# Attention, routing and mixing in one kernel: fewer idle products in the attention, the values' router products a turn later, their weights loaded in the setup, and the counts' product two steps later

## The chip, the cores and the metric

The kernel runs on one core of a Trainium2 chip. The engines have short names in all that follows: PE is TensorE (matmuls; PEld its weight loads), DVE is VectorE, ACT is ScalarE, POOL is GpSimd, SP is SyncE, which here only issues DMAs. The metric is the device time of one execution in microseconds, lower is better; the median of several runs counts.

## The reference

Three layers follow each other: an attention with a local window, a few global keys and a bias by distance; a layer of experts in which each token takes one of eight, chosen by a router, or keeps that of the token before it; and a mixer (a Fourier transform over sequence and channels, a normalization, two matmuls). Cut to what matters here:

```python
# q, k, v: (2, 8, 768, 64) f32; n_global = 8, n_local = 96
scores = (q @ k.T) / 8 + bias                 # bias = -slope[head] * distance
a = softmax(where(is_global | is_local, scores, -1e9))
x = (a @ v), heads joined to rows of 512      # (2, 768, 512)

logits = x @ w_gate                           # (2, 768, 8)
local_gate = sigmoid(x @ w_local)
for s in range(768):                          # in each sequence
    e = argmax(logits[s]) if s == 0 or local_gate[s] < 0.5 else previous e
    out[s] = softmax(logits[s])[e] * (relu(x[s] @ w1[e]) @ w2[e])

u = out + real(fft2(out));  result = u + relu(norm(u) @ w_ch1) @ w_ch2
```

## The kernel before, in words

The program issues everything by hand in a fixed order. `setup` loads the constants, `fast_attention` does the attention and, in between its work, the routing; the experts and the mixer follow. Only the attention is touched.

The sequence is cut into six tiles of 128 queries, numbered i. A unit is four heads of one sequence for one tile: 24 units, and the main loop over n starts one unit in each turn. A turn is a software pipeline over four units:

- scores of unit n (PE, L152, tile `sp`), their smallest value with the bias added (DVE, L161), the exponentials (ACT, L169);
- some idle products (PE, L50, `keep_busy`), multiplications of zeros that nobody reads, as many as the list `BUSY` says;
- transposes of unit n-1 (PE, L178, tile `tp`) in two halves, each copied out of PSUM by ACT (L184, tile `p`);
- values of unit n-2 (PE, L192, tile `op`), that is the attention's output before it is divided by the row sums;
- the division for unit n-3 (DVE, L204 to L209, `norm`).

Tile 0 sees only itself, so its scores are 128 wide and it has half the transposes and values; all later units take two tiles of keys. The buffers of `tp` are two, and idle products take one of them in turn. `op` is one.

The router's product x @ w_gate is not made from x. `prep_v` multiplies the transposed values with the router's weights (PE, L100, tiles `vt` and `wg`, into the small PSUM tile `sm`), and ACT copies the result (L103) beside the values in `vs`, so that the values product L192 gives the router's logits in ten more columns. It does so once for each tile of keys and in two halves, one for each sequence. So L192 for a tile waits for its L103.

The bias is a table that ACT writes (L229) from distances that DVE makes: eight rows 128 wide for tile 0 (`near`), eight rows 256 wide for all others (`far`).

Work beside the pipeline runs as generators: `bg.step()` stands four times in each turn and lets each live generator run on to its next `yield`. The routing of a tile (`Route.run`) is one of them: the logits, their largest, the scan over tokens that resolves "keeps the expert before" (L519), the scan that counts the tokens of each expert (L529, tile `cu`), and on PE the product of the counts (L534, `other`), from which DVE takes each token's rank (L541), PE the place (L546, L547), and POOL and SP write the rows and the list. For tile 3 the list is also read back, and a first group of tokens gathered, for an early start of the first expert (L828 and following).

A last generator halves expert weights for fast products (ACT L994, DVE L996) in some turns from 12 on.

Of the kernel before, what the change touches and what calls it, by code (L numbers as in the profile page):

```python
# [11 lines left out]
F32 = mybir.dt.float32  # L12
# [11 lines left out]
P = 128  # L24
# [3 lines left out]
NT = S // P  # L28
# [6 lines left out]
LIST = B * S  # L35
NL = E + 2
LAST = E - 1
BUSY = [6, 6, 4, 2, 2, 2, 2, 2, 2, 2] + [0] * 6
VC = D + NL + 1
BUBBLE = 0  # L40
GATE = -1.5 * 2.0 ** -23
# [4 lines left out]
def keep_busy(nc, st, ps, n):  # L46

    x = st.busy
    for _ in range(n):
        nc.tensor.matmul(ps, x[:, :1].to_broadcast([P, P]), x.unsqueeze(1).to_broadcast([P, 8, D]), start=True, stop=True)  # L50
# [10 lines left out]
def fast_attention(tc, st, io, route):  # L61
    nc = tc.nc
# [3 lines left out]
    with ExitStack() as ctx:  # L66
# [5 lines left out]
        ps_t = pool("ps_t", 2, space=PSUM)  # L72
# [15 lines left out]
        def load_v(i):  # L88
            nc.sync.dma_start(vs[:, i % KS], io["v"][i])

        def load_vt(i):
            vts[i] = raw.tile([P, HP, P], F32, name="vt", bufs=2)
            nc.sync.dma_start(vts[i], io["vT"][i])

        def prep_v(i):
            vt = vts.pop(i)
            for g in range(2):
                ps = route.sm[:, 80 + 80 * (i % 2):][:, :8 * NL]
                for k in range(4):
                    T.matmul(ps[:, k * 2 * NL:(k + 1) * 2 * NL], vt[:, 4 * g + k], route.wg[:, k, :2 * NL], start=True, stop=True)  # L100
                yield
                yield
                A.copy(vs[:, i % KS, 8 * g:8 * g + 8, D:VC - 1], ps.rearrange("p (h e) -> p h e", h=8))  # L103
                yield
            if i == 0:
                yield
                yield
                nc.sync.dma_start(gv, vs[:GMAX, 0])
# [167 lines left out]
        for n in range(N + 3):  # L276
            if ok(n):
                i, b, g = units[n]
                first = (b, g) == (0, 0)
                if (b, g) == (0, 1) and 0 < i < NT - 1:  # L280
                    load_vt(i + 1)
                if (b, g) == (1, 0) and 0 < i < NT - 1:
                    load_v(i + 1)
                if n == 1:
                    bg.add(prep_v(0))
                if i + 1 < NT and (b, g) == (1, 1):
                    bg.add(prep_v(i + 1))
                if first and i > 0:
                    load_kq(nc, st, io, i + 3)
                if (b, g) == (1, 0) and i >= 2:  # L290

                    st.ring.load(i - 2)
            if n == 1:
                bg.add(far())
            k = 4 * (n - N)
            if ok(n - 2):
                out(n - 2, 1)
            if ok(n - 3):
                norm(n - 3)
            if ok(n):  # L300
                scores(n)
                rowmin(n)
                if units[n][2]:
                    patch_k(*units[n][:2])
            step(k)
            if n < 2 * len(BUSY):
                keep_busy(nc, st, ps_t.tile([P, 2, 2, P], F32, name="tp").rearrange("p a b n -> p (a b n)"), BUSY[n // 2])
            if ok(n - 1):
                transp(n - 1, 0)
            if ok(n):  # L310
                expo(n)
            if ok(n - 1):
                out(n - 1, 0)
            step(k + 1)
            if ok(n - 1):
                transp(n - 1, 1)
            step(k + 2)
            if ok(n - 2):
                values(n - 2)
            step(k + 3)  # L320
            if ok(n - 3) and units[n - 3][2]:
                patch_v(*units[n - 3][:2])
            if n == 2:
                G.tensor_copy(gk, st.kq[0][:, 0, :, :GMAX])
            if ok(n - 3):
                live.pop(n - 3)
# [110 lines left out]
class Route:  # L437
# [3 lines left out]
    def pools(self, ctx, turn=True):  # L441
        tc = self.tc
        self.sb = ctx.enter_context(tc.tile_pool(name="rt", bufs=2))
        ps = ctx.enter_context(tc.tile_pool(name="ps_r", bufs=1, space=PSUM))
        one = ctx.enter_context(tc.tile_pool(name="rt_one", bufs=1))
        self.none = one.tile([P, (E * LIST + P) * 2 // P], I32, name="none")
        self.wg = one.tile([P, 4, 3 * NL], F32, name="wg")
        self.identb = one.tile([P, P], BF16, name="identb")
        tc.nc.scalar.dma_start(self.wg, self.io["wg"])

        self.tp = ps.tile([P, 4, P], F32, name="xtp") if turn else None
        self.sm = ps.tile([P, 512], F32, name="sm")
        return ctx.enter_context(tc.tile_pool(name="rtx", bufs=6))

    def run(self, i, xs, parts=None):
        nc, st, sb = self.tc.nc, self.st, self.sb
        V, A, G, T = nc.vector, nc.scalar, nc.gpsimd, nc.tensor
        tp, sm = self.tp, self.sm
# [71 lines left out]
                             op0=ALU.mult, op1=ALU.add)  # L530
        st.pe, st.pc = ex, cu
        yield

        T.matmul(other, from1, cu[:, P - 1:], start=i == 0, stop=True)  # L534
        if i == NT - 3:
# [218 lines left out]
def setup(tc, ctx, io):  # L754
    nc = tc.nc
    st = State()
    c = ctx.enter_context(tc.tile_pool(name="const", bufs=1))
    w = ctx.enter_context(tc.tile_pool(name="stage", bufs=1))
    st.raws = w.tile([P, PIECES, PW], F32, name="raws")
    st.raw = [st.raws[:, n] for n in range(PIECES)]  # L760

    st.kq = [t.rearrange("p (k h s) -> p k h s", k=2, h=B * H // 2) for t in st.raw]
    nn = c.tile([P, 4], I32, name="nn")
    nc.sync.dma_start(nn, io["nn"].to_broadcast([P, 4]))
    cs = c.tile([P, sum(CONSTS.values())], F32, name="consts")
    nc.scalar.dma_start(st.raw[3][:, 1024:1024 + 3 * P], io["masks"][:, :3 * P])
    nc.scalar.dma_start(cs, io["consts"])
    warm = c.tile([1, 1], F32, name="warm")
    nc.vector.memset(warm, 0.0)
    nc.scalar.activation(warm, warm, AF.Exp)  # L770
    o = 0
    for n, k in CONSTS.items():
        setattr(st, n, cs[:, o:o + k])
        o += k
    st.nf = c.tile([P, 4], F32, name="nf")
    V = nc.vector
    words = nn.rearrange("p (a b) -> p a b", b=2)
    lo, hi = st.nf[:, 0:2], st.nf[:, 2:4]
    V.tensor_copy(lo, words[:, :, 0])
    V.tensor_copy(hi, words[:, :, 1])  # L780
    V.scalar_tensor_tensor(hi, lo, 0.0, hi, op0=ALU.is_lt, op1=ALU.add)
    V.scalar_tensor_tensor(lo, hi, 2.0 ** 32, lo, op0=ALU.mult, op1=ALU.add)
    V.tensor_scalar(st.nf[:, 2:4], lo, -1.0, None, op0=ALU.mult)

    st.fast = c.tile([1, 1], I32, name="fast")
    f = c.tile([1, 2], F32, name="fastf")
    V.tensor_scalar(f[:, 0:1], st.nf[:1, 0:1], float(GMAX), None, op0=ALU.is_le)
    V.tensor_scalar(f[:, 1:2], st.nf[:1, 1:2], float(LMAX), None, op0=ALU.is_le)
    V.tensor_tensor(f[:, 0:1], f[:, 0:1], f[:, 1:2], op=ALU.mult)
    V.scalar_tensor_tensor(st.fast, st.nf[:1, 1:2], 1.0, f[:, 0:1], op0=ALU.is_ge, op1=ALU.mult)  # L790
    m = st.misc
    st.first, st.eid = m[:, 0:1], m[:16, 1:2]
    sb = c.tile([16, 4], F16, name="selbase")
    st.sb, st.sel, st.base = sb, sb[:, 0:2], sb[:, 2:4]
    st.busy = c.tile([P, D], BF16, name="busy")
    nc.gpsimd.memset(st.busy, 0.0)
    st.nch = c.tile([1, E + 2], I32, name="nch")
    st.ent0 = c.tile([P, 2], I32, name="ent0")
    st.p0 = c.tile([P, 1], F32, name="p0")
    st.ones16 = m[:16, 6:7].to_broadcast([16, P])  # L800
    st.dest = c.tile([P, B * NT, 2], I32, name="dest")
    dr = ctx.enter_context(tc.tile_pool(name="dram", bufs=1, space=DRAM))
    st.xs = dr.tile([B * S, ROW], F32, name="xs")
    st.wm = dr.tile([FT // 2, P, PW], F32, name="wmf")
    st.gv = dr.tile([GMAX, B * H, VC], F32, name="gv")
    st.list = dr.tile([E * LIST + P, 2], I32, name="list")
    st.x2 = io["x2"] if "x2" in io else dr.tile([B * S, DM], F32, name="x2")
    st.ring = Ring(tc, st, io)
    st.ring.add(w, 2)
    st.wide = w.tile([P, 3, 2, PW], F32R, name="wide")  # L810
    st.ring.slots += [[st.wide[:, k, n] for n in range(2)] for k in range(3)]

    hi, lo = st.ring.slots[4]
    v = lambda t, o, k: t[:, o:o + k * P].rearrange("p (k s) -> p k s", k=k)
    st.xe = [v(t, 0, 4) for t in (hi, lo)]
    st.he = [v(t, 4 * P, 8) for t in (hi, lo)]
    st.hs = st.raw[3][:, :1024]
    st.ye = st.raw[3][:, 1024:1024 + DM]
    return st
# [991 lines left out]
```

## Time and profile before

| | us |
|---|---|
| median of three runs | 693.82 |
| the three runs | 688.61, 693.82, 697.11 |
| the profiled execution, its own time | 695.23 |
| its span, first to last instruction | 693.5 |

The profile is that of the one execution of 695.23 us. Its times are counted from the span's start. In the attention, turn 0 begins at 6.05 and the last scores (turn 23) at 126.36; the values of turn 23's unit end at 138.2, and the experts begin at about 164. A row of the timeline gives start, length, engine, line, operation, the tiles written and read, how many instructions are merged in the row, and in brackets how long the engine stood idle before it and what released it. A matmul of full f32 stands twice in the trace for each one in the program.

### The profile page before, as it was taken

What the parts mean: (1) busy time and instruction counts of PE and PEld (TensorE: products, weight loads), DVE (VectorE), ACT (ScalarE), POOL (GpSimd) and SP (SyncE); (2) the same over time, 40 slices, a digit from 0 to 9 for tenths busy, and PEclk for the clock granted to TensorE, in tenths of its full rate; (3) what the DMA queues carried; (4) which work ended last, traced back from release to release, by engine and by line L of the source; (5) the groups of instructions that cost most, each with busy time, mean ns of one, the idle gap of its engine ahead of it and who ended that gap; (6) DMA issues with size and microseconds to landing.
All of it is one profiled execution on the core that took longest, in us unless ns stands there. A gap on an engine that the chain in (4) does not pass through costs nothing.

```text
span 693.5 us, 9885 instructions
## 1 busy us (share of the span) xinstructions
PE 657.4 (95%) x3646; PEld 538.4 (78%) x3647; DVE 392.5 (57%) x931; ACT 272.0 (39%) x478; POOL 67.8 (10%) x82
## 2 busy tenths in 40 slices
PE   7999999887989999999998899999999999999997
PEld 3778787755878899888786588777878888888885
DVE  3366766651967787877146987788742131254112
ACT  3464655611655565655243343443111131132110
POOL 0001110213034123322010000000000000000000
PEclk8799999978999999999999889999999999999999
DMA  7536545145779978995244033344110010100001
GB/s 274 219 132 131 133 116 165 50 95 187 267 264 372 318 246 277 358 342 199 89 161 176 0 122 122 121 164 160 42 61 0 1 61 0 61 0 1 0 1 61
DMA packets 26095, 96.20 MB, mean 139 GB/s; under 512 B 7764, under 2 KB 8916, under 8 KB 18096
## 3 DMA queue, kind: packets, MB, share of 16 engines
q1 hardware_dynamic: 20288, 81.19, 35.2%
q0 software_dynamic: 4736, 10.56, 4.2%
q10 hardware_dynamic: 1008, 3.65, 1.4%
q8 instruction: 34, 0.56, 0.3%
q14 instruction: 29, 0.24, 0.1%
HBM read 84.75 MB, written 14.88 MB: 144 GB/s over the span
## 4 chain that ended last, share of the span: by engine, by line
PE 40%; DVE 9%; ACT 2%; issue 1%; DVEq 0%; ACTq 0%
PE h L1621 16%; PE acc L1636 5%; PE acc L1637 5%; PE acc L1635 5%; DVE dec L1020 1%; DVE dec L1022 1%; PE y L1127 1%; PE more L1177 1%; PE acc L1442 1%; PE h L1177 1%; PE more L1127 1%; PE acc L1456 1%; PE f L1587 1%; DVE dec L1018 1%; DVE dec L1016 1%
## 5 line engine op out<-in xcount | busy, mean ns | idle before, releaser
L1626 DVE SCALAR_TENSOR_TENSOR hl<-h,hh 128x512 fp32r<-128x512 f32 x48 | 33.1, 689 | 120.4 <-ACT hh L1625 120.4
L1625 ACT ACTIVATE hh<-h 128x512 fp32r<-128x512 f32 x48 | 28.7, 597 | 156.7 <-PE h L1621 151.8
L996 DVE TENSOR_TENSOR wide<-raws,wide 128x1024 fp32r<-128x1024 f32 (+2 forms) x46 | 50.4, 1110 | 23.4 <-ACT wide L994 23.4
L169 ACT ACTIVATE t<-t,nm 128x256 f32<-128x256 f32 (+1 forms) x96 | 39.2, 479 | 43.5 <-DVE nm L161 41.6
L994 ACT CAST wide<-raws 128x1024 fp32r<-128x1024 f32 (+2 forms) x46 | 43.1, 960 | 4.4 <-PE acc L1637 3.5
L192 PE MATMUL op<-vs,p 128*128 128x75 f32 x352 | 43.9, 278 | 1.0 <-DVE xrow L209 1.0
L192 PEld LDWEIGHTS op<-vs,p 128*128 128x128 f32 x352 | 42.4, 196 | 1.2 <-issue 1.1
L161 DVE CUSTOM_DVE_ANT_0 t<-sp,bias 128x256 f32<-128x256 f32 (+1 forms) x96 | 32.9, 398 | 18.3 <-PE sp L152 15.9
L1621 PE MATMUL h<-un0h,wide 128*128 128x512 f32 (+1 forms) x136 | 42.8, 380 | 0.4 <-ACT un0h L1397 0.4
L1636 PE MATMUL acc<-wide,hh 128*128 128x512 f32 x96 | 38.1, 397 | 0.0
L1635 PE MATMUL acc<-wide,hh 128*128 128x512 f32 x96 | 37.8, 394 | 0.0
L1637 PE MATMUL acc<-wide,hl 128*128 128x512 f32 x96 | 37.7, 393 | 0.0
L1147 PE MATMUL h<-xh,wide 128*128 128x256 f32 x192 | 28.0, 281 | 2.6 <-DVE hl L1151 2.4
L1621 PEld LDWEIGHTS h<-un0h,wide 128*128 128x128 f32 x136 | 25.0, 188 | 5.8 <-ACT un0h L1397 0.6
L1007 ACT ACTIVATE dec<-raws 128x1024 f32<-128x1024 f32 x18 | 20.5, 1139 | 20.4 <-DMA wmf<-dec 6.2
L184 ACT COPY p<-tp 128x512 f32<-128x512 f32 (+1 forms) x48 | 25.1, 538 | 7.0 <-PE tp L178 6.8
L1057 POOL DMA_INDIRECT xg<-xs,ent x23 | 26.3, 1145 | 14.2 <-issue 5.5
L1147 PEld LDWEIGHTS h<-xh,wide 128*128 128x128 f32 x192 | 24.9, 188 | 3.6 <-DVE hl L1151 2.8
L178 PE MATMUL tp<-consts,t 128*128 128x128 f32 x176 | 26.8, 288 | 0.0
L178 PEld LDWEIGHTS tp<-consts,t 128*128 128x128 f32 x176 | 21.1, 147 | 6.4 <-issue 1.6
L1621 PE MATMUL h<-un0l,wide 128*128 128x512 f32 (+1 forms) x68 | 25.9, 380 | 0.0
L1150 ACT ACTIVATE hh<-h 128x512 fp32r<-128x512 f32 x28 | 16.6, 597 | 23.2 <-PE h L1147 20.4
(440 smaller groups left out, 1626.8 us busy)
## 6 DMA issues: line engine op xcount, KB each, us to landing
raws<-we SPq DMA_DIRECT2D x30, 1024.0 KB
raws<-wm SPq DMA_DIRECT2D x17, 1024.0 KB
raws<-wmf SPq DMA_DIRECT2D x7, 1024.0 KB
wmf<-dec POOLq DMA_DIRECT2D x8, 512.0 KB, 8.4
vs<-v SPq DMA_DIRECT2D x6, 600.0 KB
xs<-xrow SPq DMA_DIRECT2D x12, 260.0 KB
vt<-vT SPq DMA_DIRECT2D x6, 512.0 KB
raws<-kq SPq DMA_DIRECT2D x3, 1024.0 KB
```

The lines of the kernel that those rows point to most:

```text
L161: V.tensor_tensor_reduce(out=u.t[:, x, :u.W], in0=u.sp[:, j, k, :u.W], in1=bias[:, 4 * u.g + x, u.b0:u.b0 + u.W], scale=-0.125, scalar=3.0 ...
L169: A.activation(u.t[:, x, :u.W], u.t[:, x, :u.W], AF.Exp, bias=u.nm[:, x:x + 1], scale=-1.0)
L178: T.transpose(u.tp[k][:, j, c], u.t[:, 2 * k + j, c * P:(c + 1) * P], st.ident)
L192: T.matmul(u.op[:, x], u.p[:, x, c], vs[:, ti % KS, u.h + x], start=c == 0, stop=c == len(tiles) - 1)
L994: (first or nc.scalar.copy)(hi[:, cs], raw[:, cs])
L996: (eng() if callable(eng) else eng or nc.vector).tensor_tensor(lo[:, cs], raw[:, cs], hi[:, cs].bitcast(F32), op=ALU.subtract)
L1147: T.matmul(ps[:, u], w[:, f], x[:, k], start=n == 0, stop=n == 11)
L1621: nc.tensor.matmul(ps[:, c], a[:, k], x[:, k, c], start=n == 0, stop=n == 11)
L1626: nc.vector.scalar_tensor_tensor(hl, ps, 0.0, hh.bitcast(F32), op0=ALU.max, op1=ALU.subtract)
L1635: T.matmul(acc[c], hh[:, cs], h2, start=first, stop=False)
L1636: T.matmul(acc[c], hh[:, cs], l2, start=False, stop=False)
L1637: T.matmul(acc[c], hl[:, cs], h2, start=False, stop=last)
```

## The change

Four edits go together.

- `BUSY` had one entry for two turns: six idle products in each of turns 0 to 3, four in turns 4 and 5, two in turns 6 to 19. Now it has one for each turn: four, four, two and two in turns 0 to 3, and none behind. That is 60 before and 12 now.
- `prep_v(0)`, the router products for tile 0's values, is started in turn 2 instead of turn 1.
- The router's weights are loaded in the setup by ACT's queue, into a free part of a staging tile and ahead of the constants, and POOL copies them to `wg` once the branch to the fast attention is taken. Before, ACT's queue loaded `wg` behind that branch.
- The routing of tiles 0 to 4 yields twice more between the scan of the counts and the product of the counts. A yield is one of the four background steps of a turn.

```diff
-BUSY = [6, 6, 4, 2, 2, 2, 2, 2, 2, 2] + [0] * 6
+BUSY = [4, 4, 2, 2]
...
-                if n == 1:
+                if n == 2:
                     bg.add(prep_v(0))
...
-            if n < 2 * len(BUSY):
-                keep_busy(nc, st, ps_t.tile([P, 2, 2, P], F32, name="tp").rearrange("p a b n -> p (a b n)"), BUSY[n // 2])
+            if n < len(BUSY):
+                keep_busy(nc, st, ps_t.tile([P, 2, 2, P], F32, name="tp").rearrange("p a b n -> p (a b n)"), BUSY[n])
...
-        tc.nc.scalar.dma_start(self.wg, self.io["wg"])
+        tc.nc.gpsimd.tensor_copy(self.wg, self.st.wg)
...
         st.pe, st.pc = ex, cu
         yield
+        if i < NT - 1:
+
+            yield
+            yield
 
         T.matmul(other, from1, cu[:, P - 1:], start=i == 0, stop=True)
...
     nc.scalar.dma_start(st.raw[3][:, 1024:1024 + 3 * P], io["masks"][:, :3 * P])
+
+    st.wg = st.raw[3][:, 1024 + 3 * P:][:, :12 * NL].rearrange("p (k n) -> p k n", k=4)
+    nc.scalar.dma_start(st.wg, io["wg"])
     nc.scalar.dma_start(cs, io["consts"])
```

On PE, before, from turn 1's scores to turn 2's first idle product (tp are the transposes, sm the router products; of the idle products, six in each turn, the first stands here):

```order
L152 MATMUL sp<-raws 128x128 x4
L100 MATMUL sm<-wg,vt 128x20 x4
L50 LDWEIGHTS busy
L50 MATMUL tp<-busy 128x512
...
L178 MATMUL tp<-consts,t 128x128 x4
L100 MATMUL sm<-wg,vt 128x20 x4
L152 MATMUL sp<-raws 128x128 x4
```

The same place now, from turn 1's scores to turn 3's:

```order
L152 MATMUL sp<-raws 128x128 x4
L50 LDWEIGHTS busy
L50 MATMUL tp<-busy 128x512
...
L178 MATMUL tp<-consts,t 128x128 x4
L152 MATMUL sp<-raws 128x128 x4
L100 MATMUL sm<-wg,vt 128x20 x4
...
L178 MATMUL tp<-consts,t 128x128 x4
L192 MATMUL op<-vs,p 128x75 x4
L100 MATMUL sm<-wg,vt 128x20 x4
L152 MATMUL sp<-raws 128x128 x4
```

The first router products moved from behind turn 1's scores to behind turn 2's, with turn 0's transposes now ahead of them, and their second half from before the first values to behind them.

On ACT, before, behind turn 0's exponentials up to the second half of the router's copies (bias<-vs are table rows, t<-t,nm exponentials, p<-tp copies of transposes, vs<-sm the router's copies):

```order
L229 ACTIVATE bias<-vs 128x128 x3
L169 ACTIVATE t<-t,nm 128x128 x4
L184 COPY p<-tp 128x2x128
L229 ACTIVATE bias<-vs 128x256
L103 COPY vs<-sm 128x8x10
L229 ACTIVATE bias<-vs 128x256 x2
L184 COPY p<-tp 128x2x128
L229 ACTIVATE bias<-vs 128x256
L169 ACTIVATE t<-t,nm 128x128 x4
L184 COPY p<-tp 128x2x128
L103 COPY vs<-sm 128x8x10
```

Now, from the same place up to the first of these copies:

```order
L229 ACTIVATE bias<-vs 128x128 x3
L169 ACTIVATE t<-t,nm 128x128 x4
L184 COPY p<-tp 128x2x128
L229 ACTIVATE bias<-vs 128x256 x3
L184 COPY p<-tp 128x2x128
L229 ACTIVATE bias<-vs 128x256
L169 ACTIVATE t<-t,nm 128x128 x4
L184 COPY p<-tp 128x2x128
L229 ACTIVATE bias<-vs 128x256 x2
L103 COPY vs<-sm 128x8x10
```

The router's first copy moved from ahead of turn 2's exponentials to behind them, with all but two of the eight wide table rows ahead of it.

On PE in turn 12, the counts' product (L534 before) for tile 1, in one piece of the difference:

```order
 L152 MATMUL sp<-raws 128x256 x4
-L50 LDWEIGHTS busy
-L50 MATMUL tp<-busy 128x512
-L50 LDWEIGHTS busy
-L50 MATMUL tp<-busy 128x512
 L178 MATMUL tp<-consts,t 128x128 x4
 L528 MATMUL sm<-cu,consts 16x1
 L178 MATMUL tp<-consts,t 128x128 x4
-L534 MATMUL sm<-cu,consts 16x1
 L192 MATMUL op<-vs,p 128x75 x8
 L152 MATMUL sp<-raws 128x256 x4
```

It left its place between transposes and values; in the new program it is line L538 and stands behind the scores of turn 13, ahead of that turn's transposes. The two products of the places (L546 and L547, now L550 and L551) went from between turn 13's transposes to behind its values.

## Rows read from the trace of the kernel before

**Rows 1.** The page's 40 equal slices of the span: the granted clock, tenths.

```profile
PEclk8799999978999999999999889999999999999999
```

**Rows 2.** Timeline of PE, turn 10 and the start of turn 11.

```profile
58.13 1.13 PE L152 MATMUL sp<-raws 64*128 64x256 f32 x8
59.19 0.60 PE L50 MATMUL tp<-busy 128*128 128x512 bf16 x2
59.63 1.04 PE L178 MATMUL tp<-consts,t 128*128 128x128 f32 x8
...
62.34 1.13 PE L152 MATMUL sp<-raws 64*128 64x256 f32 x8
```

**Rows 3.** Timeline of PE, the scores of turns 22 and 23.

```profile
122.53 1.14 PE L152 MATMUL sp<-kq 64*128 64x256 f32 x8
...
126.36 1.14 PE L152 MATMUL sp<-kq 64*128 64x256 f32 x8
```

**Rows 4.** Windows of turns 21 and 22: busy by engine (count), clock, DMA, GB/s.

```profile
116.94:122.53 5.59, 5.59 (x36) 4.34 (x35) 3.48 (x17) 2.99 (x7) 1.19 (x2) 0.70 0.79 259
122.53:126.36 3.83, 3.83 (x34) 3.38 (x33) 3.76 (x20) 2.86 (x8) 1.02 (x1) 1.00 0.01 1
```

**Rows 5.** Timeline of PE, the product of the counts in tiles 0 to 4.

```profile
51.56 0.20 PE L534 MATMUL sm<-cu,consts 16*16 16x1 f32 x2 [1.45 <-ACT vs L103]
...
72.51 0.20 PE L534 MATMUL sm<-cu,consts 16*16 16x1 f32 x2 [1.18 <-ACT vs L103]
...
93.50 0.20 PE L534 MATMUL sm<-cu,consts 16*16 16x1 f32 x2 [1.18 <-ACT vs L103]
...
114.65 0.20 PE L534 MATMUL sm<-cu,consts 16*16 16x1 f32 x2 [1.57 <-ACT vs L103]
...
132.74 0.20 PE L534 MATMUL sm<-cu,consts 16*16 16x1 f32 x2 [0.80 <-DVE cu L529]
```

**Rows 6.** Timeline of ACT at the second of these.

```profile
72.24 0.22 ACT L103 COPY vs<-sm 128x80 f32<-128x80 f32 x1
```

**Rows 7.** Timeline of all engines at the start.

```profile
5.87 0.34 ACTq L449 DMA_DIRECT2D wg<-wg  x1
...
8.04 0.23 POOL L324 COPY gk<-raws 128x64 f32<-128x64 f32 x1 [7.12 <-DMA raws<-kq]
...
10.33 1.26 ACT L169 ACTIVATE t<-t,nm 128x128 f32<-128x128 f32 x4
...
11.11 1.86 PE L100 MATMUL sm<-wg,vt 128*128 128x20 f32 x8 [2.30 <-DMA vt<-vT]
...
16.00 0.37 ACT L184 COPY p<-tp 128x256 f32<-128x256 f32 x1 [4.41 <-PE tp L178]
16.27 0.42 ACT L229 ACTIVATE bias<-vs 128x256 f32<-128x256 f32 x1
16.58 0.22 ACT L103 COPY vs<-sm 128x80 f32<-128x80 f32 x1
...
16.86 1.90 PE L100 MATMUL sm<-wg,vt 128*128 128x20 f32 x8 [0.47 <-ACT vs L103]
...
18.68 1.23 PE L152 MATMUL sp<-raws 64*128 64x128 f32 x8
...
22.38 1.06 PE L178 MATMUL tp<-consts,t 128*128 128x128 f32 x4
...
23.23 1.73 PE L192 MATMUL op<-vs,p 128*128 128x75 f32 x8
```

**Rows 8.** Windows of half a microsecond where the granted clock fell and rose, columns as above.

```profile
11.00:11.50 0.50, 0.39 (x2) 0.42 (x3) 0.45 (x2) 0.50 (x3) 0.00 (x0) 0.58 0.94 395
...
24.50:25.00 0.50, 0.50 (x5) 0.42 (x4) 0.00 (x0) 0.50 (x2) 0.00 (x0) 0.76 0.10 19
```

**Rows 9.** Timeline of PE, scores of turn 4, and of turn 21 at the low clock.

```profile
30.04 1.13 PE L152 MATMUL sp<-raws 64*128 64x256 f32 x8
...
116.94 2.08 PE L152 MATMUL sp<-kq 64*128 64x256 f32 x8
```

## The prediction, made before the changed kernel ran

> **What bounds the kernel now.** I read the page's slices first, then TensorE's (PE's) timeline through the attention turn by turn, then the windows of the same turns, then the waits, and last the start with all engines. A turn is one pass of the loop over n; the attention's turns 0 to 23 each start four heads. The slices show a clock that is near full except at the very start, around the fifth part of the span and at a few later places [rows 1]. Within the attention PE has hardly a gap: a plain turn is scores, two idle products, transposes, values, and the next scores follow at once, 4.21 us in all, of which the two idle products take 59.19 to 59.63, 0.44 us or 0.22 each [rows 2]. Turns from 20 on have no idle products already, and turn 22, the same work without them, takes 3.83 us [rows 3]; its window shows the clock at 1.00 (the 2.4 GHz level) and VectorE (DVE) busy 3.76 us of the 3.83 [rows 4]. So an idle product here is on the path, and what comes next behind PE is close.
>
> The second thing on PE's path is five waits, one per tile of queries, each before the product of the counts at L534: 1.45, 1.18, 1.18, 1.57 and 0.80 us [rows 5]. The row that ends the second is ScalarE's (ACT's) copy L103, which stands in its queue behind the four exponentials and a copy out of PSUM and ends at 72.46, just before 72.51 [rows 6]; the last is ended by the scan itself. After the fourth wait the granted clock of turn 21 is 0.70 and the turn takes 5.59 us [rows 4].
>
> The third is the start. PE stands still for 2.30 us before the first router product at 11.11 [rows 7], since the transposed values must land first; the granted clock drops there to the 1.2 GHz level and comes back at 24.7 [rows 8]. First values only at 23.23 [rows 7], and turn 4 begins at 30.04 [rows 9].
>
> **Idle products from turn 4 on.** Turns 4 and 5 lose four each, turns 6 to 19 two each: 36 x 0.22 = 7.9 us [rows 2]. The check is turn 22 against turn 10: 4.21 - 3.83 = 0.38 for two [rows 2, 3]. Nothing on PE hides them.
>
> **The counts' wait.** Two more background steps put the product behind the next turn's scores, some 2 us later on PE, and the longest wait was 1.57. What is queued behind it on PE (values, the next scores) no longer waits; what waits for it is the rank on DVE, the positions, the writes of rows and list, and these have turns to spare, except for tile 3, whose list feeds the early gather. For that one the early product's transposes stand some three turns and a half behind the positions, and they were not waited for before, so I cost it at nothing. Sum of the five waits: 6.2 us [rows 5]. With the fourth goes the slow stretch behind it: 5.59 - 3.83 = 1.76 for turn 21 against turn 22, of which I take 1.7, since turn 21 holds two small products more [rows 4].
>
> So turns 4 to 23 give 7.9 + 6.2 + 1.7 = 15.8 us. Behind them everything (the last route, the gathers, the experts) starts from the last values and moves along with them, so I carry the gain to the end undiminished.
>
> **The router's weights in the setup.** The issue of 0.34 us leaves ACT's queue behind the branch [rows 7] and stands before it, where ACT has nothing but the table load; 60 KB go ahead of the constants. GpSimd (POOL) copies them, which by the nearest copy is 0.23 us [rows 7], long before the first router product. I cost all this at nothing, with an end of 0.3 on either side: the first scores may see their keys a little later, and the first transposed values may land a little earlier. The Trainium skill, SBUF — State Buffer, section "Who interferes with whom", says that a VectorE instruction with two operands in SBUF and a GpSimd one that reads SBUF block each other; the copy now falls on the first mask operations, and by that rule the first bias would come up to that copy's length later. No run here shows it, and I leave it in the 0.3.
>
> **The start.** PE no longer meets the router products in turn 1, so it goes on with turn 0's transposes and turn 2's scores. But what sets the first values now is ACT. Its queue up to turn 1's exponentials is the same as before, and these end at 10.33 + 1.26 = 11.59 [rows 7]. Behind them stand, in the new order: copy, three tables, copy, a table, turn 2's four exponentials, copy, two tables, and the router's copy for which the first values wait. By the starts at 16.00, 16.27 and 16.58 a copy holds ACT 0.27 us and a table 0.31; the exponentials 1.26; the last copy 0.22 [rows 7]. 11.59 + 3 x 0.27 + 6 x 0.31 + 1.26 + 0.22 = 15.7. PE's own work is done some 2.3 us before (its last transposes follow the second copy, at about 13.1, and take a few tenths), so PE stands still about as long as the 2.30 us after which the clock fell before [rows 7, 8]. I therefore expect the clock to fall again, only about 3 us later, and price the rest of turns 2 and 3 at the low level, from rows at that level: values 1.73, router 1.90, scores 1.23, router 1.90, two idle products 0.88 (twice their 0.44), transposes 1.06, values 1.73, router 1.90 [rows 2, 7], together 12.3. Turn 4 then begins at 28.0 instead of 30.04, 2.0 us earlier [rows 9].
>
> Where the clock comes back is the unknown. Before, it rose when PE had run idle products, transposes and values without a gap; behind turn 20 it rose at the end of a scores and transposes stretch. In the changed kernel router and value products fill most of turns 2 and 3, so I place it in turn 4 or 5, the first with scores at full width. At the low level turn 4 costs 2.08 + 1.06 + 1.73 = 4.9 us [rows 7, 9], half of it too much, 2.4; turn 5 has twice the transposes, 5.9, and 3.0 too much. I take half of the 5.4, 2.7. The start then gives 2.0 - 2.7 = -0.7. Bounds: if the clock never falls, the 12.3 become 6.2, turn 4 begins 8.1 earlier and nothing is lost, +8.1; if it comes back only behind turn 7, the two turns more cost 3.8 each (below), 2.0 - 5.4 - 7.6 = -11.0.
>
> **The sum.** 15.8 - 0.7 = 15.1 us. Against the profiled execution's own 695.23 that is 680.1; that execution is 1.4 over the median of the three runs, 693.82, so the median should come to 678.7, say 679. A measurement of this kernel can tell about 2% from no change, here 13.9 us or 679.9: the forecast lies almost on that line.
>
> **Rivals.**
> *The clock stays up at the start* (or is back at once). For: the wait is broken by two idle products and two transposes. Against: the fall behind 2.30 us. Gain 15.8 + 8.1 = 23.9, median 670. Chance 0.13.
> *DVE becomes the bound.* It is busy 3.76 of 3.83 us in turn 22, and turns with routing hold as much [rows 4]. If the idle products only filled time that DVE needs, turns 4 to 19 do not shrink and only the waits and the slow turn go: 6.2 + 1.7 - 0.7 = 7.2, median 686.6. Against: turn 22 itself has that DVE load and is short. Chance 0.14.
> *The clock does not hold without the idle products* (the side of slower). They were the dense work between weight loads; without them a short wait may let the clock fall again and again in turns 6 to 19, where before three waits of over a microsecond passed without a fall. A plain turn at the low level is 2.08 + 2 x 1.06 + 2 x 1.73 = 7.7 us against 3.83, so 3.8 are lost for each; from the fourth such turn on the change is slower than before, and eight give 709. For: turn 21. Against: turns 22 and 23 run at 1.00 with none, and the waits that went ahead of a fall are what the change removes. Chance 0.12, of which 0.05 over 2% slower. The Trainium skill, TensorE: Matmul & The Clock Gate, Part 4 (PE-mode transpose), says that transposes do not count as busy work for the clock in the way that products do; by that rule this rival would be the likeliest, with about a quarter of each turn's work not counting. The trace does not bear it out: turn 22 has the same transposes, no idle product, and the full clock [rows 4].
> *Anything else,* such as a transfer of keys or weights that is late for shorter turns: 0.03.
>
> **How the numbers follow.** The forecast has 0.58; its own range is 675 to 684, by the ends of the clock's return between the end of turn 3 and the end of turn 5. The range 671 to 688 takes in most of the first two rivals and leaves out the far ends of the first and the third. Faster by over 2%: 0.13 and six tenths of 0.58, 0.48. Slower by over 2%: 0.05. Within: 0.47.
>
> **What would show it.** Turn 10 should take about 3.8 us; no wait of over 0.3 us before the counts' product; first values at about 15.7 behind a wait of 2 us for ACT's copy; a granted clock of 0.5 from about 14 to about 32; turn 4 at 28 and the last scores about 14 us earlier than 126.36 [rows 3]. I am wrong if plain turns stay over 4 us, if a new wait stands in front of values or transposes, or if the clock is low in any stretch between turns 6 and 19.

## The result and the profile after

The changed kernel takes 687.58 us, median of 18 runs (682.17 to 690.39), against 694.81 us for the kernel before on the same chips (18 runs): a ratio of 0.9893, 95% interval 0.9871 to 0.9916. It is 7.2 us faster; 15 were forecast. The profiled execution took 690.13 us, 5.1 less than that of before, with a span of 688.3.

The page's slices of the changed kernel, which answer to [rows 1]: the start's low slice, the second, stands at 5 where it stood at 7, and the tail's low slice comes one earlier, at 6 where it was 7.

```profile
PEclk9599999688999999999998899999999999999999
```

PE's timeline of the changed kernel at the start (start, length, line, tiles, in brackets the idle time before and what ended it), for [rows 7, 9]:

```profile
7.09 0.71 PE L152 MATMUL sp<-raws 64*128 64x128 f32 x8 [1.10 <-DMA raws<-kq]
...
13.09 0.66 PE L178 MATMUL tp<-consts,t 128*128 128x128 f32 x4
15.71 1.93 PE L192 MATMUL op<-vs,p 128*128 128x75 f32 x8 [1.97 <-ACT vs L103]
...
27.11 2.08 PE L152 MATMUL sp<-raws 64*128 64x256 f32 x8
...
36.85 1.14 PE L152 MATMUL sp<-raws 64*128 64x256 f32 x8
```

The first values stand at 15.71 behind a wait of 1.97 us for ACT's copy, as forecast (15.7, some 2 us); turn 4 begins at 27.11 (forecast 28.0). The windows where the clock fell and rose (busy time of each engine, clock third from the end), for [rows 8]:

```profile
15.50:16.00 0.50, 0.29 (x2) 0.29 (x2) 0.00 (x0) 0.50 (x4) 0.00 (x0) 0.80 1.16 479
36.00:36.50 0.50, 0.50 (x5) 0.50 (x5) 0.00 (x0) 0.50 (x2) 0.00 (x0) 0.72 0.12 13
```

So the 1.2 GHz level held from 15.8 to 36.3, 20.5 us, where before it was 13.7 [rows 8]. From there to 125.0 the clock is at 1.00. The plain turn 10, for [rows 2]:

```profile
54.38 1.13 PE L152 MATMUL sp<-raws 64*128 64x256 f32 x8
55.44 1.09 PE L178 MATMUL tp<-consts,t 128*128 128x128 f32 x8
56.37 1.91 PE L192 MATMUL op<-vs,p 128*128 128x75 f32 x16
58.21 1.13 PE L152 MATMUL sp<-raws 64*128 64x256 f32 x8
```

It takes 3.83 us, as forecast, and no wait stands before any product of the counts (L538 now, which answers to [rows 5]). But turn 15, which holds routing, takes 6.65 us, more than the 6.17 of before. PE, DVE and ACT there:

```profile
78.83 0.22 PE L509 MATMUL sm<-identb,gf 128*16 128x128 bf16 x1 [0.20 <-DVE gf L504]
...
83.00 1.07 PE L100 MATMUL sm<-wg,vt 128*128 128x20 f32 x8 [0.29 <-DVE su L521]
84.00 0.49 PE L152 MATMUL sp<-raws,kq 64*128 64x128 f32 x4
```

```profile
82.48 0.47 DVE L519 TENSOR_TENSOR_SCAN ex<-rows,ex,sm 16x128 f32<-16x128 f32 x1 [1.20 <-ACT vs L103]
```

```profile
80.00 1.71 ACT L169 ACTIVATE t<-t,nm 128x256 f32<-128x256 f32 x4 [1.16 <-DVE nm L161]
```

PE waits twice for DVE here, 0.20 us before L509 and 0.29 before L100, the second time behind the scan over tokens (L521 follows it). The scan waits for ACT, whose copies follow the exponentials, and the exponentials wait for DVE's row minima (L161): they begin 2.65 us into the turn, where it was 1.65 before.

Turn 12 holds a wait that none of the three kernels without the added steps has there. PE, and the issue that it waits for:

```profile
67.48 1.98 PE L192 MATMUL op<-vs,p 128*128 128x75 f32 x16 [0.72 <-DMA vs<-gv]
```

```profile
63.27 0.28 SPq L129 DMA_DIRECT2D vs<-gv  x1
```

The values of unit 10 wait for a DMA (the patch L129, which puts the global keys' values into a tile's first rows); before, the wait of 1.18 us for the counts [rows 5] stood in this turn. All eleven kernels with the added steps have the new wait, of 0.57 to 2.11 us. Then the tail. PE from turn 23's scores ([rows 3] before) to the experts' first transposes:

```profile
116.08 1.13 PE L152 MATMUL sp<-kq 64*128 64x256 f32 x8
...
125.40 3.67 PE L192 MATMUL op<-vs,p 128*128 128x75 f32 x16 [2.75 <-DMA vs<-gv]
...
130.19 3.66 PE L192 MATMUL op<-vs,p 128*128 128x75 f32 x16 [0.98 <-DVE xrow L209]
...
159.99 1.94 PE L1096 MATMUL xtp<-consts,xg 128*128 128x128 f32 x8 [3.24 <-issue]
```

The scores of turn 23 come 10.3 us earlier than before, but the values of unit 22 now wait 2.75 us for another such patch, and behind that wait the clock is low:

```profile
125.50:141.50 16.00, 13.37 (x52) 11.14 (x52) 8.05 (x35) 1.05 (x3) 3.62 (x3) 0.50 0.35 117
```

The low stretch lasts from 125.0 to 142.1, 17.1 us. The clock was low in this part before, too, but later and for 10.2 us, from 137.4 to 147.6. Why the patch is late shows in POOL's and SP's DMA issues (SPq and POOL rows, same columns) and in SP's waits (who, for what, us in total, times, longest):

```profile
117.87 0.97 POOL L559 DMA_INDIRECT list<-dest,pos  x1 [0.30 <-issue]
```

```profile
111.23 0.81 SPq L558 DMA_DIRECT2D xs<-xrow  x2
122.77 0.33 SPq L570 DMA_DIRECT2D ent<-list  x1
123.20 1.13 SPq L129 DMA_DIRECT2D vs<-gv  x2
```

```profile
SPq L570 <- DMA list<-dest,pos: 10.6, 1, 10.6
```

SP stands 10.6 us at L570, the read-back of tile 3's list, until POOL's last write of the list, issued by 118.84, has landed. The patch is next in the same queue. In the kernel before the same read-back (L566) held SP for nearly as long:

```profile
SPq L566 <- DMA list<-dest,pos: 10.0, 1, 10.0
```

```profile
127.09 0.33 SPq L566 DMA_DIRECT2D ent<-list  x1
```

```profile
132.87 2.01 PE L192 MATMUL op<-vs,p 128*128 128x75 f32 x16
```

But there it was over 0.7 us behind turn 23's scores (127.09 against 126.36), 5.8 us ahead of unit 22's values; now it is over 6.7 us behind them (122.77 against 116.08). From turn 23's scores to the experts' first transposes it now takes 43.9 us.

### The profile page after: what moved, and what is told of

It is laid out like the page before. It is cut to its first block, busy times and chain, and to the rows that moved or that the text cites. A ratio compares the mean times of both kernels' runs of the same rounds, so it can differ in the third digit from the quotient of the medians.

```text
span 688.3 us, 9803 instructions
## 1 busy us (share of the span) xinstructions
PE 653.5 (95%) x3598; PEld 540.1 (78%) x3599; DVE 391.4 (57%) x931; ACT 271.3 (39%) x478; POOL 71.2 (10%) x83
## 4 chain that ended last, share of the span: by engine, by line
PE 41%; DVE 9%; ACT 2%; issue 1%; DVEq 0%; ACTq 0%
PE h L1628 16%; PE acc L1643 5%; PE acc L1644 5%; PE acc L1642 5%; DVE dec L1027 1%; DVE dec L1029 1%; PE y L1134 1%; PE acc L1463 1%; PE acc L1449 1%; PE more L1184 1%; PE h L1184 1%; PE more L1134 1%; DVE dec L1025 1%; PE f L1594 1%; DVE dec L1023 1%
## 5 line engine op out<-in xcount | busy, mean ns | idle before, releaser
L192 PE MATMUL op<-vs,p 128*128 128x75 f32 x352 | 48.8, 298 | 7.0 <-DMA vs<-gv 3.5
L192 PEld LDWEIGHTS op<-vs,p 128*128 128x128 f32 x352 | 47.3, 215 | 8.1 <-issue 4.0
L161 DVE CUSTOM_DVE_ANT_0 t<-sp,bias 128x256 f32<-128x256 f32 (+1 forms) x96 | 32.9, 398 | 13.8 <-PE sp L152 12.3
L1014 ACT ACTIVATE dec<-raws 128x1024 f32<-128x1024 f32 x18 | 20.5, 1139 | 26.3 <-issue 15.0
L1064 POOL DMA_INDIRECT xg<-xs,ent x23 | 29.0, 1260 | 15.2 <-issue 6.1
```

What stands on the lines that cost most here:

```text
L161: V.tensor_tensor_reduce(out=u.t[:, x, :u.W], in0=u.sp[:, j, k, :u.W], in1=bias[:, 4 * u.g + x, u.b0:u.b0 + u.W], scale=-0.125, scalar=3.0 ...
L192: T.matmul(u.op[:, x], u.p[:, x, c], vs[:, ti % KS, u.h + x], start=c == 0, stop=c == len(tiles) - 1)
```

## The experiments

Three stretches of each profiled kernel tell where time went: the start of turn 6 (the whole start), turn 6 to turn 23 (steady turns), and turn 23 to the experts' first transposes (tail). They are differences of rows such as those above, from one execution of each kernel. "Ratio" is to the kernel before on the same chip, with its 95% interval. The medians come from several chips, whose medians of the kernel before lie between 692.20 and 694.81, so that a difference between medians of two chips is good to some 3 us only.

| kernel | turn 6 at | turns 6 to 23 | tail | median | ratio |
|---|---|---|---|---|---|
| before | 37.17 | 89.19 | 37.63 | 694.81 | |
| changed | 36.85 | 79.23 | 43.91 | 687.58 | 0.9893 (0.9871 to 0.9916) |
| changed, again | 35.22 | 81.28 | 41.47 | 688.38 | 0.9928 (0.9899 to 0.9958) |
| tile 3 without the two steps | 36.79 | 84.29 | 36.62 | 687.65 | 0.9934 (0.9900 to 0.9967) |
| read-back on POOL | 33.63 | 81.40 | 39.62 | 683.23 | 0.9880 (0.9819 to 0.9941) |
| before, read-back on POOL | 35.19 | 90.70 | 36.49 | 692.79 | 0.9993 (0.9959 to 1.0027) |
| before, two steps alone | 32.35 | 82.29 | 43.62 | 692.69 | 0.9974 (0.9931 to 1.0017) |
| wait at the start filled | 27.58 | 79.07 | 44.19 | 680.33 | 0.9832 (0.9793 to 0.9870) |
| filled, read-back on POOL | 27.51 | 79.98 | 40.39 | 676.23 | 0.9769 (0.9722 to 0.9817) |
| weights behind the branch | 34.88 | 80.68 | 44.19 | 688.95 | 0.9946 (0.9915 to 0.9976) |
| idle products back | 33.28 | 83.91 | 42.18 | 691.78 | 0.9983 (0.9952 to 1.0013) |
| same products behind the wait | 32.70 | 79.27 | 42.66 | 686.49 | 0.9903 (0.9869 to 0.9936) |
| one step in tile 3 | 27.50 | 80.28 | 36.48 | 675.16 | 0.9760 (0.9724 to 0.9796) |
| before, wait filled | 31.26 | 93.85 | 39.06 | 692.96 | 0.9993 (0.9961 to 1.0025) |

**Tile 3 without the two added steps.**

```diff
-        if i < NT - 1:
+        if i < NT - 1 and i != NT - 3:
```

> The changed kernel without the two added steps in tile 3 alone; in tiles 0, 1, 2 and 4 they stay. Theory A (in tile 3 the later list makes SP's queue stand on the list's read-back, and the patches of the values behind it come late; the values of unit 22 wait 2.75 us and the granted clock falls): that wait goes and the clock does not fall at 125, which gives back about 6 us (the 6.0 us that the stretch from turn 23's scores to the early expert's first product is longer than before), while the fourth wait before the product of the counts returns with 1.6 us, or 3.3 with a slow turn behind it: 683 to 685 us. Theory B (the two steps are harmless, the clock falls at the end for want of the idle products): the fall at 125 stays and the wait returns, 689 to 691 us.

Measured 687.65: neither theory's time. PE's rows:

```profile
107.74 0.20 PE L538 MATMUL sm<-cu,consts 16*16 16x1 f32 x2 [1.57 <-ACT vs L103]
...
108.10 3.70 PE L192 MATMUL op<-vs,p 128*128 128x75 f32 x16
111.72 2.08 PE L152 MATMUL sp<-kq 64*128 64x256 f32 x8
...
117.25 1.13 PE L152 MATMUL sp<-kq 64*128 64x256 f32 x8
...
126.87 1.98 PE L192 MATMUL op<-vs,p 128*128 128x75 f32 x16 [0.15 <-PE tp L178]
```

The mechanism of theory A is there: the wait before unit 22's values is gone, the clock did not fall at 125 (it fell at 131.9 and was low for 6.8 us, where the changed kernel has 17.1), and the tail is 36.6 us, 1.0 less than in the kernel before. What I had too small was the price on the other side: the 1.57 us wait returned and the clock fell behind it, so that the steady turns are 5.1 us longer (84.29 against 79.23). In tile 3 the two steps trade one wait for another.

**The read-back on POOL's queue,** in the changed kernel and in the kernel before.

```diff
-            nc.sync.dma_start(st.ent0, st.list[1:P + 1])
+            nc.gpsimd.dma_start(st.ent0, st.list[1:P + 1])
```

> The changed kernel with all its added steps, but the read-back of the list is issued by GpSimd's queue instead of SP's, so the patches no longer stand behind it. Theory A: no wait for the patch before the values of unit 22, no fall of the clock there, 6 us less than the changed kernel, 681 to 682 us. Theory B: 687.6 us within one, the clock low from 125 as before. If GpSimd's own later work is held by the read, the early gather comes later but nothing else.

> The kernel before with that read on GpSimd's queue and nothing else. Theory A: there the patches were behind the read too, but no value waited for them, so 694.8 us within one. If it gains several us as well, the block on SP's queue was paid before the change too, and is not what ate the gain.

In the changed kernel the wait is gone with the steps still in:

```profile
121.74 1.98 PE L192 MATMUL op<-vs,p 128*128 128x75 f32 x16 [0.15 <-PE tp L178]
...
129.76 1.12 PE L835 MATMUL tp<-consts,vs 128*128 128x128 f32 x4 [1.91 <-DMA vs<-xs,ent]
```

The tail is 4.3 us shorter and the median 4.4 lower than the changed kernel's, 683.23. Theory A had 6 and no fall of the clock: some of it went to the early gather, for which PE now waits 1.91 us at 129.76, and the clock fell all the same, at 125.7 for 10.2 us. The times alone do not settle the gain: the interval of this ratio overlaps that of the changed kernel, and in the pair on one chip below the medians (680.33 and 676.23) differ by 4.1, but the six runs of each overlap. What the fourteen profiles show is plain: the seven kernels with two steps in tile 3 and the read-back on SP have a wait of 2.3 to 3.1 us for the patch and a tail of 41.5 to 44.2 us, the seven others no such wait and 36.5 to 40.4. In the kernel before the move is worth nothing (0.9993), as expected: SP stood at the read-back there too, but no value waited for what was behind it. What came with the change is the wait, not the block on SP's queue.

The Trainium skill, DMA: Bandwidth & Descriptors, section "Issuing engines are not separate DMA queues", says that a DMA begun by another engine saves only the issuing sequencer's time, which it calls usually small. The trace agrees as far as the issue goes, which took 0.33 us (122.77); but the move also took away the 10.6 us for which SP stood waiting ahead of that issue.

**The two steps alone, in the kernel before.**

```diff
         st.pe, st.pc = ex, cu
         yield
+        if i < NT - 1:
+
+            yield
+            yield
```

> The kernel before with the two added steps in the routing and nothing else. By the prediction's sum the five waits (6.2 us) and the slow turn (1.7) go: 687 us. Theory A: the waits go, but the patch comes late in the last turns and takes about 6 back: 692 to 694 us, with a wait of 2 us or more before the values of unit 22 and a low clock behind it. Theory B: 687 us, no such wait.

Measured 692.69, as theory A had it. The steady turns lost 6.9 us (89.19 to 82.29), close to the prediction's 7.1 for them (6.2 + 1.7 less the 0.80 of tile 4, whose wait lies behind turn 23); the tail grew by 6.0, with the wait and the low clock in the same place:

```profile
123.94 3.66 PE L192 MATMUL op<-vs,p 128*128 128x75 f32 x16 [2.73 <-DMA vs<-gv]
```

Theory B falls here: all idle products of before are in this kernel, and the clock fell near 124 all the same.

**Idle products in the wait at the start,** nine, between turn 2's last transposes and the first values.

```diff
             step(k + 2)
+            if n == 2:
+                keep_busy(nc, st, ps_s.tile([P, 2, 2, 256], F32, name="sp")[:, 0].rearrange("p u n -> p (u n)"), 9)
             if ok(n - 2):
```

> The changed kernel with nine more idle products in turn 2, between its last transposes and the first values, where PE stood still for 1.97 us. Theory C (the clock falls at 15.8 because of that wait, and stays low for 20.5 us): the products fill the wait, the granted clock stays at 1.00, turn 4 begins near 22 instead of 27.1 and turn 6 near 28.6 instead of 36.9; about 8 us less than the changed kernel, 679 to 680 us. Rival (the work of turns 2 to 5 is set by ACT's and DVE's chain and the clock falls anyway): 687.6 us within one, turn 6 near 37.

> Both edits: the nine idle products before the first values, and the list's read-back on GpSimd's queue. If the block on SP's queue (theory A, worth 4 to 5 us) and the fall of the clock at the start (theory C, worth about 8) are separate losses, they add: 674 to 676 us. If one makes the other, or the gain of the start is used up by a later wait, not below 679 us.

```profile
13.53 2.11 PE L50 MATMUL sp<-busy 128*128 128x512 bf16 x9
15.74 1.11 PE L192 MATMUL op<-vs,p 128*128 128x75 f32 x8
...
21.90 1.13 PE L152 MATMUL sp<-raws 64*128 64x256 f32 x8
```

The first values start at 15.74, 0.03 later than with the wait open, and the clock never fell there. Its mean from 11 to 116 us is 1.00:

```profile
11.00:116.00 105.00, 98.47 (x841) 84.86 (x839) 72.87 (x383) 72.55 (x185) 11.46 (x21) 1.00 0.56 169
```

Turn 4 begins at 21.90 and turn 6 at 27.58; 680.33 us, 7.3 less than the changed kernel by the medians, 4.2 by the ratios, and 8.6 less than the version with the weights behind the branch (below), which ran on the same chip. Theory C holds in time and place for the changed kernel. With the read-back on POOL as well the median is 676.23 (forecast 674 to 676): the gains seem to add, as far as six runs tell.

**The same nine products behind the wait,** in turn 3.

```diff
-BUSY = [4, 4, 2, 2]
+BUSY = [4, 4, 2, 11]
```

> The changed kernel with the same nine more idle products, but in turn 3, behind the first values, so that the 1.97 us wait stays open. Theory C (the wait itself makes the clock fall): it falls at 15.8 as before, the nine cost 0.22 to 0.44 us each, 2 to 4 us, and the time is 687 to 692 us, less only if they bring the clock back sooner. Rival (it is the amount of dense work around turn 2 that counts, not the wait): the clock stays up or is back within a few us, 680 to 682 us as with the products in the wait.

```profile
15.70 1.11 PE L192 MATMUL op<-vs,p 128*128 128x75 f32 x8 [2.04 <-ACT vs L103]
...
20.61 4.29 PE L50 MATMUL tp<-busy 128*128 128x512 bf16 x11
...
27.03 1.13 PE L152 MATMUL sp<-raws 64*128 64x256 f32 x8
```

```profile
17.50:24.50 7.00, 7.00 (x28) 4.26 (x28) 1.22 (x9) 1.28 (x4) 0.00 (x0) 0.52 0.84 348
```

The clock fell behind the wait, at about 17.4 here, and was back at 24.2; 686.49 us, little under the changed kernel on the same chip (688.38), and not told apart from it. Nine of the eleven products cost 3.5 us, most of it at the low level, and seem to have brought the clock back sooner; a gain clear of the scatter came only where the products stood in the wait.

**The weights behind the branch again.**

```diff
-        tc.nc.gpsimd.tensor_copy(self.wg, self.st.wg)
+        tc.nc.scalar.dma_start(self.wg, self.io["wg"])
...
-    st.wg = st.raw[3][:, 1024 + 3 * P:][:, :12 * NL].rearrange("p (k n) -> p k n", k=4)
-    nc.scalar.dma_start(st.wg, io["wg"])
```

> The changed kernel with the router's weights loaded where they were before, by ACT's queue behind the branch, and all else as changed. PE's first scores come at 6.0 to 6.1 us instead of 7.09. If that is carried to the end, 686.5 us; if the first values, which wait for ACT's chain at 15.7, take no notice, 687.6 us. The prediction had this edit at nothing within 0.3.

```profile
6.39 0.71 PE L152 MATMUL sp<-raws 64*128 64x128 f32 x8 [0.95 <-DMA raws<-kq]
...
15.93 1.99 PE L192 MATMUL op<-vs,p 128*128 128x75 f32 x8 [2.05 <-ACT vs L103]
```

The scores came 0.7 us earlier, the first values 0.2 later, and the median is 688.95: no gain, so the 1.0 us that the first scores lost in the changed kernel (7.09 against 6.05) is not where the time went.

**The later idle products back in the changed kernel.**

```diff
-BUSY = [4, 4, 2, 2]
+BUSY = [4, 4, 2, 2, 4, 4] + [2] * 14
```

> The changed kernel with four idle products in each of turns 4 and 5 again and two in each of turns 6 to 19, as before. By the prediction's sum 36 x 0.22 = 7.9 us slower, 695.5 us. By the rival that DVE is next behind PE, turns without them are already held elsewhere in part: 3 to 5 us slower, 691 to 692.5 us; by that one the turns with routing (11, 15, 19) stay as long as they are without, 6.1 to 6.7 us. A third way: the clock comes back earlier than 36.3 with them, and some of the loss is paid for.

Measured 691.78: 4.2 us slower than the changed kernel by the medians, 6.2 by the ratios, and 2.8 slower than the version with the weights behind the branch on the same chip. That leans to the rival's 3 to 5, but the times alone do not rule out 7.9. Of the rival's detail turn 11 held (6.17 us with the products, 6.12 without); turn 15 was even shorter with them (6.17 against 6.65). Turn 19 took 6.84, and turn 20 5.62, with another fall of the clock at its start:

```profile
103.42 1.93 PE L152 MATMUL sp<-kq 64*128 64x256 f32 x8
...
109.04 1.13 PE L152 MATMUL sp<-kq 64*128 64x256 f32 x8
```

Idle products up to turn 19 did not keep the clock up there. The clean pair for them is the kernel with the two steps alone against the changed kernel, neither of which has a fall in these turns: 82.29 - 79.23 = 3.1 us for 28 products, where 28 x 0.22 = 6.2 were reckoned. Plain turns give 0.35 to 0.40 each, and so does turn 7 with the routing of tile 0; turns 11, 15 and 19, which hold the routing of the next tiles, give 0.05, -0.47 and -0.47, and turn 18 -0.22. Turn 12 gives 0.73.

**The changed kernel again, and one step in tile 3** on top of the filled wait and the read-back on POOL.

```diff
             yield
-            yield
+            if i != NT - 3:
+                yield
```

> The changed kernel itself once more, to stand on the same chip as the next three and to see how much its start differs from run to run. 687.6 us within 2, a ratio near 0.989; the clock falls near 15.8 behind the 2 us wait in its profile too, and comes back anywhere between 30 and 37 (the runs so far: 30.1 to 36.3).

> The version with the filled wait and the read-back on GpSimd's queue, and one added step instead of two in tile 3. The product of the counts then stands behind the values of the same turn, so its wait stays hidden, and the list is ready one step earlier; the early gather, for which PE waited 3.6 us with two steps, comes about 1 us earlier: 675 us against 676. If the wait of tile 3 returns with a slow turn, 678 us or more.

The changed kernel gave 688.38, with the wait for the patch in the tail at 2.29 us and two falls of the clock in turns 16 and 20 that the first profile did not have. The version with one step:

```profile
101.89 0.17 PE L553 MATMUL sm<-selbase,rk 16*128 16x2 f16 x1 [1.10 <-DVE rk L548]
...
120.28 1.12 PE L838 MATMUL tp<-consts,vs 128*128 128x128 f32 x4 [1.24 <-DMA vs<-xs,ent]
...
144.26 1.95 PE L1099 MATMUL xtp<-consts,xg 128*128 128x128 f32 x8 [3.44 <-DMA xg<-xs,ent]
```

The wait for the early gather fell from the 3.59 us of the version with two steps to 1.24, and a wait of 1.10 for the rank came in turn 21. At 675.16 it is the fastest version, 2.4% under the kernel before, though not told apart from the 676.23 with two steps.

**The kernel before with its first wait filled.**

```diff
                 if units[n][2]:
                     patch_k(*units[n][:2])
+            if n == 1:
+                keep_busy(nc, st, ps_t.tile([P, 2, 2, P], F32, name="tp").rearrange("p a b n -> p (a b n)"), 10)
             step(k)
```

> The kernel before with ten idle products in turn 1 between the scores and the first router product, where PE stood still for 2.30 us, and nothing else. Theory C: the clock does not fall at 11 and the 13.7 us at the low level go; the start gains up to 6 us by the rows, less the runs in which it comes back early by itself: 688 to 691 us. If the loss at the start belonged to the change alone, 694 us within one.

A miss: 692.96, a ratio of 0.9993. In the profile the start did what theory C says (clock 1.00 from 7 to 40, turn 6 at 31.26), but the clock then fell behind the first wait for the counts, which the profile of before had passed without a fall:

```profile
45.65 0.20 PE L536 MATMUL sm<-cu,consts 16*16 16x1 f32 x2 [1.45 <-ACT vs L103]
```

```profile
47.00:53.50 6.50, 6.50 (x31) 4.72 (x29) 2.49 (x13) 2.27 (x6) 0.90 (x2) 0.50 0.23 84
```

Turns 6 to 23 took 93.85 us. Whether that happens in most runs of it, one profile can't say. The kernel before with the read-back on POOL, with its start as it was, has a fall behind the same wait too (clock low from 51.9 to 55.3). Why the start's gain does not reach the median stays open.

## Why the prediction fell short

The measured 687.58 lies at the edge of the stated range (671 to 688), outside the forecast's own (675 to 684). That it is near the 686.6 of the rival "DVE becomes the bound" is luck: that rival had no gain from the idle products and no loss in the tail.

**Right:** the place of the first values and their wait, the fall of the clock behind it and turn 4 (27.11 against 28.0), plain turns of 3.83 us, no wait before the counts' product, and the worth of the waits (6.9 us in the steady turns of the kernel with the two steps alone). The weights' load brought the first scores 0.7 us later, more than the 0.3 allowed, but the first values, which wait for ACT, took no notice. The rival that the clock does not hold without idle products did not come about as a rule: 105 us at 1.00 with none behind turn 3. By the rule that the prediction cites there from the Trainium skill, TensorE: Matmul & The Clock Gate, Part 4 (PE-mode transpose), this rival would have been the likeliest; the row of the filled version, with transposes in every turn, does not bear that out here. Single falls did come in some profiles without the products (turns 16 and 20 of the changed kernel's second one, at 1.5 us each, turn 13 with the read-back on POOL, turn 16 with that and the filled wait), which the prediction had named as a sign of being wrong, and one also with the products in.

**The step that failed** is in the part on the counts' wait: for tile 3, "whose list feeds the early gather", I cost the later list at nothing, looking only at who reads the gathered tokens, and then carried the gain "to the end undiminished". SP's queue was not looked through: the list's read-back stands in it ahead of two patches on which the next values wait. With the two steps that became a wait of 2.75 us and a longer stretch at the low clock; the tail grew by 6.3 us (37.63 to 43.91), where I had counted on 0.8 less. That is 7.1 of the 11.1 us by which the profile at the experts' start (163.99 to 159.99, 4.0 earlier) falls short of 15.1. Without the two steps in tile 3 the tail is 36.62, the 0.8 less that was counted on and a little more. Taking the read-back out of SP's queue returned 3.8 to 4.3 us of the tail in the profiles; much of the rest is the gather itself, which is not free either: with the queue clear PE waits 1.91 and 3.59 us for it.

The wait for a patch in turn 12 (0.72 us where one of 1.18 was removed) is a smaller case that was not priced either: there the patch was not held up, its issue came 1.1 us ahead of the turn's scores (0.7 before), but the values came 3.1 us behind them instead of 4.1, too soon for it. A new wait in front of values was among the signs of being wrong that the prediction names. What came lies nearest to "a transfer of keys or weights that is late for shorter turns", which had a chance of 0.03.

**Mis-sized:** the idle products. A plain turn gives 0.38 for two, not 0.44; in turns 11, 15 and 19, which hold routing, the rival of DVE next in line was right, as a chain: row minima on DVE, exponentials and copies on ACT, the scan on DVE, PE behind it. 28 of them gave 3.1 us of 6.2. That is the loss in the steady turns, where 9.96 were measured against 13.2 reckoned (6.2, four waits of together 5.4, and 1.7).

**Not settled:** the start as a whole. The clock came back at the end of turn 5 (36.3), where the forecast had counted on half of turns 4 and 5. But the term of -0.7 lies within the start's scatter: turn 6 began at 37.17, 35.19 and 32.35 in three profiles with the start of before, and at 36.85, 36.79, 35.22 and 33.63 in four with the changed one. That the wait is what costs in the changed kernel is shown by filling it: turn 6 then began at 27.58 and 27.51. In the kernel before, filling its wait brought turn 6 to 31.26 in one profile and nothing in the median.

## What to carry to other kernels

When a step is moved later, follow every DMA that it issues into its queue and read what stands behind it: a transfer that has to wait before it is issued holds up one behind it that the next matmul needs. A short wait on PE costs more than its length when the clock falls behind it, so price both sides of a trade at the low level, and try products in a wait that can't be removed rather than elsewhere; it paid in the changed kernel and not in the one before, so measure it. Taking out an idle product gains its length only in turns where nothing else stands close behind PE.

## What the runs showed of the hardware

- The same instructions left the low level after very different times. With the start of before it held 13.7 us in one profile, about 10 in a second and about 3 in a third; with the changed start 20.5 in two, about 17 in another and about 14 in a fourth.
- Equal waits were followed by a fall in some profiles and not in others. The first of [rows 5], of 1.45 us, passed without one; the same wait of 1.45 us at 45.65 in the kernel before with its first wait filled did not. In turn 12 a wait of 1.89 us was followed by a fall (read-back on POOL) and one of 2.11 was not (weights behind the branch). In the second profile of the changed kernel the clock was at 0.50 from 83 to 86 with no wait over 0.3 us in turn 15 ahead of it.
- From the end of POOL's last issue of the list (118.84) to the start of SP's read of it (122.77) passed 3.9 us.
